# Long filter and two dense layers on one core: the second step in pairs of octets

## The chip, the cores and the metric

The kernel runs on one core of a Trainium2 chip. The metric is the device time of one execution in microseconds, lower is better. Before the change the median of 3 runs is 1322.25 us (1322.2 to 1323.78).

## The reference

A long convolution by FFT over 12480 positions and 128 channels, a gate with x, and then two dense layers on the 12480 tokens (128 to 2048 to 128). Cut to what matters:

```python
h_filt = (np.maximum(pos_emb @ w1, 0.0) @ w2) * np.exp(-0.01 * pos)[:, None]   # filter, 64 rows to 128 channels
y = irfft(rfft(x * v, 2 * S) * rfft(h_filt, 2 * S))[:S]                          # causal convolution
x = x * y
h = x @ w_in;  x = (h * np.clip(h + 3, 0, 6) / 6) @ w_out                        # first dense layer
h = x @ w_in2; x = np.where(h > 0, h, np.exp(np.minimum(h, 0)) - 1) @ w_out2     # second dense layer
```

The weights come as 64-bit floats; the kernel converts them to 32 bits itself.

## The kernel before, in words

**The four steps of the convolution.** The transform has length 179 x 128 and is done in four steps of small matrix products. The first step makes spectra along 98 rows, for 32 groups of channels of the signal (`first_u`) and 16 groups of filter rows (`first_r`). The second step works on 90 frequencies k, in octets: `OCTETS` has 11 octets of 8 and a last one of 2. The third (`third_main`, `third_rest`) and the fourth step (`fourth`, 17 blocks) go back to positions. From about 251 us on the two dense layers run, in units of 512 tokens by 256 hidden columns, and fill the rest of the time.

**The second step, per octet o.** `second_r(o)` (line 450): eight 128x128 products on TensorE turn the filter rows by the table `gm`, and ScalarE copies the result back (line 455). `second_h(o)` (line 457): the filter rows, 64 wide, are expanded to 128 channels by `w2`: two products of 64 contraction rows for each k, into two PSUM buffers `hr[0]` and `hr[1]`; ScalarE copies each (line 466) and makes a negated third copy (line 467) into `hss[o % 2]`. `second_u(o, hf)` (line 469): for each half hf of the channels, eight 128x128 products turn the signal's spectrum by the same table into one PSUM buffer `z`. `second(o, hf, z)` (line 478): VectorE makes two products of z with the expanded filter (line 487) into a pair of buffers of `mms`; GpSimd adds the two (line 492) back into the spectrum. `mms` has two such pairs, used in turn.

**PSUM.** `bank(name, shape, tag)` gives a buffer of 128 x 1024 floats under one of two tags, "px" and "py", each with two buffers in turn. In the second step `second_r` and `second_h` use "px" and `second_u` uses "py". A `second_h` takes both buffers of its tag.

**Tables.** `load_gm0(n)` requests a table group of four k on SP's queue into one of eight places; an octet has two groups, so four octets' tables are present.

**The weight conversion.** `weight_steps` is a generator with 34 steps: the first requests three raw blocks, the second begins block 0, and each of the 32 others finishes one block k. Such a step is three VectorE operations (clamp, line 289; lines 291 and 292), one on GpSimd (line 295), a request for block k+3 on SP (line 262), two ScalarE operations that begin block k+1 (lines 277 and 278), and a store of block k-1 on ScalarE's queue (line 272). `convert(n)` adds n to a counter and issues a step for each whole one. Three steps come in the first step of the transform, 18 in the second, four in the third and nine in the fourth. In `second` the call stands between the two products and their sum. In the third and fourth step a raw request is held until the next `bunch` and goes out behind its other requests.

**Order.** The schedule is written out by hand: each engine executes in the order of the program text. There is no planner.

Of the kernel before, what the change touches and what calls it, by code (L numbers as in the profile page):

```python
# [18 lines left out]
S, D, FO, FF = 12480, 128, 64, 2048  # L19

ZERO = 10398
N1, N2 = 179, 128
# [113 lines left out]
def tile_kernel(ctx, tc, xc, vc, xT, posT, w1_d, w2_d, moe_w, t1_d, gm_d, cs_d, ti_d, rows_d, column_d, ratio_d, outT):  # L136
# [11 lines left out]
    def bank(name, shape, tag=None):  # L148
        if tag is None:
            turn[0] += 1  # L150
            tag = "px" if turn[0] % 2 else "py"
        return ps.tile(shape, F32, tag=tag, name=name)
# [9 lines left out]
    OCT = 8  # L162
# [61 lines left out]
    GN = 8  # L224
# [75 lines left out]
        store(len(jobs) - 1)  # L300

    weights = weight_steps(JOBS, cut(cv, 2 * WC, 3), cut(cv[:, 6 * WC:], WC, 2), cut(cv[:, 8 * WC:], WC, 4))
    RATE = (0.75, 0.65)
    due = [0.0]

    def convert(n):
        due[0] += n
        while due[0] >= 1:
            due[0] -= 1
            next(weights, None)  # L310
# [18 lines left out]
    NC = D // DC  # L329
# [90 lines left out]
    for kind, n in order:  # L420
        if kind:
            first_r(n)
            if n == NR // 2:
                nc.sync.dma_start(cs, cs_d)
                nc.sync.dma_start(w2s, w2_d)
            if n in GM_AT:
                load_gm0(GM_AT.index(n))
        else:
            first_u(us.pop(0), n)
            if n + LOOK < NC:  # L430
                us.append(signal(n + LOOK))
            convert(n >= NC - 3)
    load_gm0(GN - 1)
    lctx.close()
    bctx = ctx.enter_context(ExitStack())
# [11 lines left out]
    def gm_of(k):  # L447
        return gms[k // KC % GN][:, k % KC]

    def second_r(o):  # L450
        k0, nk = OCTETS[o]
        r = bank("r", [128, OCT, N2], "px")
        for j in range(nk):
            nc.tensor.matmul(r[:, j], lhsT=Rk[:, k0 + j], rhs=gm_of(k0 + j), start=True, stop=True)  # L454
        nc.scalar.copy(Rk[:, k0:k0 + nk], r[:, :nk])

    def second_h(o):
        k0, nk = OCTETS[o]
        hr = [bank("h", [128, OCT, D], "px") for r in range(2)]
        for j in range(nk):  # L460
            for r in range(2):
                p = slice(r * FO, (r + 1) * FO)
                nc.tensor.matmul(hr[r][:, j], lhsT=Rk[p, k0 + j], rhs=w2s[p], start=True, stop=True)  # L463
        hs = hss[o % 2]
        for r in range(2):
            nc.scalar.copy(hs[:, :nk, r], hr[r][:, :nk])
        nc.scalar.mul(hs[:, :nk, 2], hs[:, :nk, 1], -1.0)

    def second_u(o, hf, tag="py"):
        k0, nk = OCTETS[o]  # L470
        z = bank("z", [128, OCT, D], tag)
        for j in range(nk):
            nc.tensor.matmul(z[:, j], lhsT=gm_of(k0 + j), rhs=spectrum(hf, k0 + j, 1)[:, :, 0], start=True, stop=True)  # L473
        return z
# [3 lines left out]
    def second(o, hf, z, size=OCT, rate=0):  # L478
        k0, nk = OCTETS[o]
        for a in range(0, nk, size):  # L480
            n = min(size, nk - a)
            m1, m2 = (m[products[0] % 2][:, :, :n] for m in mms)
            products[0] += 1
            h = hss[o % 2][:, a:a + n, :, hf * HD:(hf + 1) * HD]
            flat = h[:, :, 0].unsqueeze(3).to_broadcast([128, n, HD, 2])
            for mm, h in ((m1, flat), (m2, h[:, :, 1:].rearrange("p k r d -> p k d r"))):
                nc.vector.tensor_tensor(  # L487
                    out=mm.rearrange("p d k r -> p k d r"),
                    in0=z[:, a:a + n].rearrange("p k (d r) -> p k d r", r=2), in1=h, op=ALU.mult,
                )  # L490
            convert(rate)
            nc.gpsimd.tensor_tensor(  # L492
                out=spectrum(hf, k0 + a, n), in0=m1, in1=m2[:, :, :, ::-1], op=ALU.add
            )

    def third_main(hf, s0, n, tag=None):
        q = bank("q", [128, 2, 4 * N2], tag)
        for j in range(n):
            for r in range(2):
                for p in range(2):  # L500
                    mm = nc.tensor.matmul(  # L501
                        q[p * HD:(p + 1) * HD, r, j * HN:(j + 1) * HN], lhsT=AuM[hf][:, s0 + j, :, r], rhs=csr[:, r, p],
                        start=True, stop=True,
                    )
                    if j <= 4:
                        anchor[0] = mm
        qs = half(q, n * HN)
        for o, op in enumerate((ALU.subtract, ALU.add)):
            nc.vector.tensor_tensor(
                out=main[hf][:, o, :, s0:s0 + n].rearrange("p g e t -> p e g t"),  # L510
                in0=q[:, 0, :n * HN].rearrange("p (e g t) -> p e g t", e=n, t=2),
                in1=qs.rearrange("p (e g t) -> p e g t", e=n, t=2), op=op,
            )
# [44 lines left out]

    mains = groups([8] * 8)
    turn[0] = 1  # L560
    for o in range(2):
        second_r(o)
        convert(1)
    for o in range(last + 1):
        if o == 0:
            z = second_u(o, 0)
            second_h(o)
            convert(1)
        else:
            second_h(o)  # L570
            z = second_u(o, 0)
        if 0 < o < last:
            second_r(o + 1)
        rate = RATE[0] if o < last - 1 else 0
        second(o, 0, z, rate=rate)
        if o == last:
            third_main(1, *mains[0], "px")
        second(o, 1, second_u(o, 1), rate=rate)
        for n in range(2 * (o > 0)):
            load_gm0(2 * (o - 1) + GN + n)  # L580
    bctx.close()
    lds = cctx.enter_context(tc.tile_pool(name="ldi", bufs=1, reuse_waits="tile"))
    held[0] = True
# [169 lines left out]
    for i, banks in enumerate(BATCHES):  # L753
        if i < len(ahead):
            y, parts, widths = ahead[i]
        else:
            y = new_y(i)
            parts, widths = fourth(i, y)
            parts[0]()
        parts[1]()  # L760
        if bunches.get(i) or i in bunches and pending:
            bunch(*bunches[i])
        o = START.get((banks[0][0], 1), 0)
        if len(set(widths)) == 1:
            n, w = len(widths), widths[0]
            z = xp[:, o:o + n * w].rearrange("p (b n) -> p b n", n=w)
            nc.vector.tensor_tensor(out=z, in0=y[:, :n, :w], in1=z, op=ALU.mult)
        else:
            for b, w in enumerate(widths):
                nc.vector.tensor_tensor(out=xp[:, o:o + w], in0=y[:, b, :w], in1=xp[:, o:o + w], op=ALU.mult)  # L770
                o += w
        if i == 2:
            nc.scalar.copy(x0[:, 0], xp[:, :TT])
        if i in (13, 14, 15):
            split_w(*early[i - 13])
        if i == 3:
            nc.vector.tensor_tensor(out=x0[:, 1], in0=xp[:, :TT], in1=x0[:, 0].bitcast(F32), op=ALU.subtract)
        if i < 15:
            convert(RATE[1])
    assert next(weights, "done") == "done"  # L780
    cctx.close()
    wp = ctx.enter_context(tc.tile_pool(name="wp", bufs=1, reuse_waits="tile"))
# [211 lines left out]
```

## Time and profile before

| what | us |
|---|---|
| median of 3 runs | 1322.25 |
| the profiled execution | 1321.99 |
| its span, first to last instruction | 1320.2 |
| TensorE busy | 1312.2 (99%) |
| VectorE busy | 1134.5 (86%) |
| ScalarE busy | 1006.0 (76%) |
| GpSimd busy | 411.7 (31%) |

The granted TensorE clock is 1.00 in all stretches read here. In the trace PE is TensorE's products and PEld its weight loads, DVE is VectorE, ACT ScalarE, POOL GpSimd, and SPq the queue of requests on SP. A float32 product appears as two instructions. The end of a PE instruction is modelled, so groups of products are best placed by the starts of their weight loads. A part in square brackets is idle time of the engine before the row and what ended it.

### The profile page before, as it was taken

Reading aid. Unit: us, or ns where it says so; the run is one execution under the profiler, and the core shown is the slowest. Engines: PE = TensorE matmul, PEld = TensorE weight load, DVE = VectorE, ACT = ScalarE, POOL = GpSimd, SP = SyncE. Lnnn points to the kernel's source line nnn. Section 1 sums busy time; section 2 is a strip of 40 time slices with the busy share of each in tenths; the row PEclk is TensorE's granted clock in tenths of the full one; section 3 lists DMA queues with packets and bytes.
Section 4 is the critical chain, followed back from the end, with each engine's and each line's share of the span. In section 5 each row is a group of like instructions: output and inputs, shape, how many; then the busy total and the mean of one; then the engine's idle time right before and its main releaser. Section 6 shows DMA issues by size and latency. Waiting matters only on the chain.

```text
span 1320.2 us, 23005 instructions
## 1 busy us (share of the span) xinstructions
PE 1312.2 (99%) x9184; PEld 1127.2 (85%) x9184; DVE 1134.5 (86%) x1209; ACT 1006.0 (76%) x1210; POOL 411.7 (31%) x319
## 2 busy tenths in 40 slices
PE   9999999999999999999999999999999999999998
PEld 9999999888888888888888888888888888888898
DVE  6769877789988888888888888888888888898897
ACT  5677663588877888788877887788778878887776
POOL 1027741334222222333222222222223233222223
PEclk9999999999999999999999999999999999999999
DMA  8944447510000000000000000000000000000000
GB/s 266 266 129 148 133 141 236 180 48 17 9 8 6 4 8 8 9 1 9 9 9 0 8 9 8 1 9 8 8 1 9 8 9 1 8 8 9 8 9 12
DMA packets 33676, 58.80 MB, mean 45 GB/s; under 512 B 3962, under 2 KB 10272, under 8 KB 33568
## 3 DMA queue, kind: packets, MB, share of 16 engines
q1 hardware_dynamic: 28816, 53.07, 13.2%
q10 hardware_dynamic: 4752, 4.26, 0.9%
q8 instruction: 72, 1.18, 0.4%
q14 instruction: 36, 0.29, 0.1%
HBM read 46.73 MB, written 10.58 MB: 43 GB/s over the span
## 4 chain that ended last, share of the span: by engine, by line
PE 92%; DVE 2%; issue 2%; DMA 1%; ACT 1%; POOL 1%; SPq 0%; ACTq 0%; POOLq 0%; DVEq 0%
PE h L867 39%; PE o L911 39%; PE pa L401 4%; PE y L677 3%; PE z L473 2%; PE q L501 2%; PE r L454 1%; PE h L463 1%; PE q L539 1%; DMA uv<-in_xc 1%; DMA qb<-in_posT 0%; POOL a L880 0%; DVE qb L487 0%; ACT gs L896 0%; DVE au L487 0%
## 5 line engine op out<-in xcount | busy, mean ns | idle before, releaser
L911 PE MATMUL o<-gs,w 128*128 128x512 f32 (+1 forms) x2400 | 566.0, 384 | 0.9 <-POOL w L814 0.5
L911 PEld LDWEIGHTS o<-gs,w 128*128 128x128 f32 x2400 | 445.1, 188 | 86.7 <-DVE gs L901 1.0
L880 POOL TENSOR_SCALAR a<-a 128x1024 f32<-128x1024 f32 (+1 forms) x200 | 295.9, 1480 | 706.7 <-ACT a L879 706.5
L901 DVE TENSOR_TENSOR gs<-g,gs 128x1024 fp32r<-128x1024 f32 (+1 forms) x400 | 482.2, 1205 | 5.3 <-ACT gs L896 4.5
L896 ACT CAST gs<-g 128x1024 fp32r<-128x1024 f32 (+1 forms) x400 | 410.1, 1025 | 52.7 <-DVE g L888 51.3
L888 DVE SCALAR_TENSOR_TENSOR g<-a,h 128x1024 f32<-128x1024 f32 (+1 forms) x200 | 238.8, 1194 | 117.5 <-ACT a L877 117.2
L867 PE MATMUL h<-x,w 128*128 128x512 f32 (+1 forms) x1200 | 298.1, 384 | 0.2 <-ACT a L879 0.2
L867 PE MATMUL h<-xs,w 128*128 128x512 f32 (+1 forms) x1200 | 297.9, 384 | 0.0
L879 ACT ACTIVATE a<-h 128x1024 f32<-128x1024 f32 (+1 forms) x200 | 201.4, 1007 | 89.6 <-PE h L867 88.3
L867 PEld LDWEIGHTS h<-xs,w 128*128 128x128 f32 x1200 | 223.1, 188 | 44.7 <-DVE g L888 0.4
L867 PEld LDWEIGHTS h<-x,w 128*128 128x128 f32 x1200 | 223.0, 188 | 43.7 <-issue 0.5
L877 ACT ACTIVATE a<-h,bounds 128x1024 f32<-128x1024 f32 (+1 forms) x200 | 219.0, 1095 | 50.3 <-PE h L867 50.3
L890 DVE SCALAR_TENSOR_TENSOR g<-a,h 128x1024 f32<-128x1024 f32 (+1 forms) x200 | 237.6, 1188 | 0.2 <-POOL a L880 0.2
L295 POOL TENSOR_TENSOR cv<-cv 128x256 int32<-128x256 int32 x32 | 23.4, 732 | 121.0 <-DVE cv L292 111.8
L401 PE MATMUL pa<-tab,qb 98*64 98x180 f32 x512 | 41.6, 316 | 0.1
L401 PEld LDWEIGHTS pa<-tab,qb 98*64 98x64 f32 x512 | 37.8, 138 | 2.6 <-ACT qb L405 0.4
L277 ACT ACTIVATE cv<-cv 128x256 int32<-128x256 uint32 x32 | 14.3, 446 | 23.7 <-DMA cv<-in_mw 17.7
L814 POOL TENSOR_TENSOR w<-w 128x256 fp32r<-128x256 f32 x26 | 19.2, 742 | 37.9 <-DVE gs L901 16.7
L677 PE MATMUL y<-qb 128*64 128x97 f32 (+3 forms) x896 | 30.9, 248 | 0.1
L677 PEld LDWEIGHTS y<-qb 128*64 128x64 f32 (+1 forms) x896 | 28.9, 137 | 1.9 <-issue 0.3
L492 POOL TENSOR_TENSOR qb<-qb,bp 128x1024 f32<-128x1024 f32 (+1 forms) x12 | 26.9, 2240 | 3.9 <-DVE bp L487 3.9
L843 ACT COPY y<-o 128x512 f32<-128x512 f32 (+1 forms) x25 | 14.5, 578 | 17.5 <-PE o L911 17.5
(98 smaller groups left out, 866.1 us busy)
## 6 DMA issues: line engine op xcount, KB each, us to landing
cv<-in_mw SPq DMA_DIRECT2D x32, 256.0 KB
uv<-in_xc SPq DMA_DIRECT2D x32, 196.0 KB
out_T<-y SPq DMA_DIRECT2D x23, 256.0 KB
qb<-in_gm SPq DMA_DIRECT2D x22, 256.0 KB
au<-in_xT SPq DMA_DIRECT2D x16, 268.0 KB
qb<-in_ti SPq DMA_DIRECT2D x14, 294.0 KB
w_scratch<-cv ACTq DMA_DIRECT2D x32, 128.0 KB
w<-w_scratch SPq DMA_DIRECT2D x16, 256.0 KB
```

The lines of the kernel that those rows point to most:

```text
L401: nc.tensor.matmul(pa[f * HN:(f + 1) * HN, j, :2 * NK], lhsT=src(j, f), rhs=table[:, f], start=True, stop=True)
L492: nc.gpsimd.tensor_tensor(out=spectrum(hf, k0 + a, n), in0=m1, in1=m2[:, :, :, ::-1], op=ALU.add)
L677: anchor[0] = nc.tensor.matmul(y[c * HD:(c + 1) * HD, b, off:off + w], lhsT=lhsT, rhs=rhs[:, H1 - w:], start=(b, c) in fresh, stop=done, s ...
L867: nc.tensor.matmul(h[:, j], lhsT=wslice(2 * m - 2, a, 2 * u + j), rhs=x[:, b], start=i == 0, stop=i == 2)
L877: paced[0] = nc.scalar.activation(a, h, AF.Relu, bias=three)
L879: nc.scalar.activation(a, h, AF.Exp)
L880: nc.gpsimd.tensor_scalar(a, a, 1.0, 0.0, op0=ALU.min, op1=ALU.max)
L888: last_dve[0] = nc.vector.scalar_tensor_tensor(g, a, 6.0, h, op0=ALU.min, op1=ALU.mult)
L890: last_dve[0] = nc.vector.scalar_tensor_tensor(g, a, -1.0, h, op0=ALU.add, op1=ALU.max)
L896: nc.scalar.copy(t[:, 0], g)
L901: last_dve[0] = nc.vector.tensor_tensor(out=t[:, 1], in0=g, in1=t[:, 0].bitcast(F32), op=ALU.subtract)
L911: nc.tensor.matmul(o[:, :WID[t]], lhsT=wslice(2 * m - 1, a, 2 * u + j), rhs=gs[:, b, j], start=u == 0 and j == 0 and i == 0, stop=u == NU ...
```

## The change

The octets of the second step are taken in pairs (a, a+1). Both `second_h` come first, one in each tag, then four `second_u` with their `second`; `second_r(a+2)` comes after the first two of them and `second_r(a+3)` after the last. The tags change places from pair to pair: a = 0, 4, 8 have p = "px" and q = "py", a = 2, 6, 10 the reverse. The last pair consists of octet 10 and the short octet 11. The requests for the tables of octets a+4 and a+5 follow the octet whose places they take. The conversion steps are dealt out anew: five in the first step, 15 in the second (none, one or a third at the end of a pair), four in the third and ten in the fourth.

```diff
-    RATE = (0.75, 0.65)
+    RATE = 0.67
@@ first step
-            convert(n >= NC - 3)
+            convert(n >= NC - 5)
@@ second step: second_r, second_h and second_u take their tag as an argument
-    for o in range(2):
-        second_r(o)
-        convert(1)
-    for o in range(last + 1):
-        if o == 0:
-            z = second_u(o, 0)
-            second_h(o)
-            convert(1)
-        else:
-            second_h(o)
-            z = second_u(o, 0)
-        if 0 < o < last:
-            second_r(o + 1)
-        rate = RATE[0] if o < last - 1 else 0
-        second(o, 0, z, rate=rate)
-        if o == last:
-            third_main(1, *mains[0], "px")
-        second(o, 1, second_u(o, 1), rate=rate)
-        for n in range(2 * (o > 0)):
-            load_gm0(2 * (o - 1) + GN + n)
+    tags = ("px", "py")
+    for o in range(2):
+        second_r(o, tags[o])
+        convert(1)
+
+    def load_tables(o):
+        for n in range(2):
+            load_gm0(2 * o + n)
+
+    for a in range(0, last, 2):
+        p, q = tags[::1 - (a & 2)]
+        second_h(a, p)
+        convert(a == 0)
+        second_h(a + 1, q)
+        convert(1 if a + 1 < last else 0)
+        second(a, 0, second_u(a, 0, p))
+        second(a, 1, second_u(a, 1, p), rate=1 if a + 1 < last else 0)
+        load_tables(a + 4)
+        if a + 1 < last:
+            second_r(a + 2, q)
+            second(a + 1, 0, second_u(a + 1, 0, q))
+            z = second_u(a + 1, 1, p)
+            second_r(a + 3, p)
+            second(a + 1, 1, z)
+            convert(a in (2, 6))
+            load_tables(a + 5)
+    second(last, 0, second_u(last, 0, "px"))
+    third_main(1, *mains[0], "px")
+    second(last, 1, second_u(last, 1, "py"))
@@ fourth step
-            convert(RATE[1])
+            convert(RATE)
```

## Rows read from the trace of the kernel before

**Rows 1.** Busy time by stretch: us, busy (count) per engine, granted clock, DMA.

```profile
102.50:156.00 53.50, 53.50 (x564) 51.74 (x563) 48.38 (x60) 36.24 (x49) 41.98 (x26) 1.00 0.48 148
300.00:1320.20 1020.20, 1016.38 (x4593) 851.41 (x4591) 898.18 (x812) 811.54 (x863) 299.61 (x206) 1.00 0.02 7
```

**Rows 2.** Timeline of weight loads, octet 4: start, duration, engine, line, operation.

```profile
112.05 1.86 PEld L463 LDWEIGHTS h<-qb 64*128 64x128 f32 x32
114.03 1.90 PEld L473 LDWEIGHTS z<-qb 128*128 128x128 f32 x16
115.85 1.86 PEld L454 LDWEIGHTS r<-qb 128*128 128x128 f32 x16
117.64 1.89 PEld L473 LDWEIGHTS z<-au,qb 128*128 128x128 f32 x16
119.66 1.86 PEld L463 LDWEIGHTS h<-qb 64*128 64x128 f32 x32
```

**Rows 3.** Timeline of VectorE and GpSimd around octets 4 and 5.

```profile
114.06 2.38 POOL L492 TENSOR_TENSOR qb<-qb,bp 128x1024 f32<-128x1024 f32 x1
...
115.43 1.17 DVE L289 TENSOR_SCALAR cv<-cv 128x256 f32<-128x256 f32 x1
...
118.23 2.38 POOL L492 TENSOR_TENSOR au<-qb,au 128x1024 f32<-128x1024 f32 x1
...
120.64 1.23 DVE L487 TENSOR_TENSOR qb<-z,qb 128x1024 f32<-128x1024 f32 x1 [0.95 <-POOL au L492]
...
121.79 1.25 DVE L487 TENSOR_TENSOR au<-z,qb 128x1024 f32<-128x1024 f32 x1
122.95 0.29 DVE L289 TENSOR_SCALAR cv<-cv 128x256 f32<-128x256 f32 x1
...
123.60 0.43 DVE L292 SCALAR_TENSOR_TENSOR cv<-cv 128x256 int32<-128x256 int32 x1
...
124.17 0.73 POOL L295 TENSOR_TENSOR cv<-cv 128x256 int32<-128x256 int32 x1 [1.23 <-DVE cv L292]
```

**Rows 4.** Timeline: a product behind its `second_u`, and `second_u` behind a product.

```profile
136.90 2.09 PE L473 MATMUL z<-qb 128*128 128x128 f32 x16
...
139.13 1.23 DVE L487 TENSOR_TENSOR qb<-z,bp 128x1024 f32<-128x1024 f32 x1 [0.17 <-PE z L473]
...
166.63 1.24 DVE L487 TENSOR_TENSOR au<-z,qb 128x1024 f32<-128x1024 f32 x1
...
167.92 0.53 PEld L473 LDWEIGHTS z<-au,qb 128*128 128x128 f32 x4 [0.50 <-DVE au L487]
```

**Rows 5.** Timeline of ScalarE and of TensorE's waits, first octets.

```profile
78.11 0.43 ACT L277 ACTIVATE cv<-cv 128x256 int32<-128x256 uint32 x1
...
78.92 0.82 ACT L405 ACTIVATE au<-pa 128x512 f32<-128x512 f32 x2
...
80.60 1.01 ACT L455 COPY qb<-r 128x1024 f32<-128x1024 f32 x1
...
86.18 1.93 ACT L466 COPY qb<-h 128x1024 f32<-128x1024 f32 x2 [1.77 <-PE h L463]
...
88.14 1.06 ACT L467 ACTIVATE qb<-qb 128x1024 f32<-128x1024 f32 x1
...
90.53 1.90 PEld L473 LDWEIGHTS z<-qb 128*128 128x128 f32 x16 [0.52 <-DVE bp L487]
...
100.61 1.86 PEld L454 LDWEIGHTS r<-qb 128*128 128x128 f32 x16 [0.56 <-ACT qb L466]
```

**Rows 6.** Timeline where the fourth step meets the dense layers.

```profile
246.31 0.44 ACT L277 ACTIVATE cv<-cv 128x256 int32<-128x256 uint32 x1 [4.93 <-DMA cv<-in_mw]
...
247.99 1.43 DVE L292 SCALAR_TENSOR_TENSOR cv<-cv 128x256 int32<-128x256 int32 x1
...
249.34 1.83 DVE L767 TENSOR_TENSOR au<-y,au 128x780 f32<-128x780 f32 x2
...
254.31 2.59 DVE L888 SCALAR_TENSOR_TENSOR g<-a,h 128x1024 f32<-128x1024 f32 x2 [1.04 <-ACT a L877]
...
255.58 1.22 PEld L867 LDWEIGHTS h<-xs,w 128*128 128x128 f32 x6 [0.16 <-DVE g L888]
```

More of the change, by code (lines that the diff above doesn't have):

```diff
@@ L448, in gm_of, with second_r @@
         return gms[k // KC % GN][:, k % KC]
-    def second_r(o):
+    def second_r(o, tag):
         k0, nk = OCTETS[o]
-        r = bank("r", [128, OCT, N2], "px")
+        r = bank("r", [128, OCT, N2], tag)
         for j in range(nk):
@@ L455, in second_r, with second_h @@
         nc.scalar.copy(Rk[:, k0:k0 + nk], r[:, :nk])
-    def second_h(o):
+    def second_h(o, tag):
         k0, nk = OCTETS[o]
-        hr = [bank("h", [128, OCT, D], "px") for r in range(2)]
+        hr = [bank("h", [128, OCT, D], tag) for r in range(2)]
         for j in range(nk):
@@ L467, in second_h, with second_u @@
         nc.scalar.mul(hs[:, :nk, 2], hs[:, :nk, 1], -1.0)
-    def second_u(o, hf, tag="py"):
+    def second_u(o, hf, tag):
         k0, nk = OCTETS[o]
```

## The prediction

> **What bounds the kernel now.** I read the busy time by stretch first. In seven middle octets of the second step TensorE is busy all 53.5 us of 53.5, VectorE 48.4, GpSimd 42.0; in the dense layers from 300 us on TensorE is busy 1016.4 of 1020.2 [rows 1]. The reader is to see two things: TensorE sets the time on both sides of the change, so each microsecond it loses or gains here reaches the end; and VectorE has only a tenth to spare beside it.
>
> Second the timeline of one octet, by the starts of TensorE's weight loads [rows 2]. `second_h` takes 1.98 us, `second_u` 1.82, `second_r` 1.79, the other `second_u` 2.02: 7.61 together. The same 16 products of `second_u` cost 0.20 more when `second_h` follows, and `second_h` itself, whose loads span 1.86, lasts 0.12 to 0.14 longer until the next group starts. So the change between 128-row and 64-row products costs about 0.34 us an octet.
>
> Third VectorE and GpSimd in the same octet [rows 3]. Products stand 1.15 and 1.16 us apart. One waits 0.95 us for a GpSimd sum: the two buffer sets of `mms` alternate, so a product waits for the sum of two products earlier, which takes 2.38. A conversion step queues between a product and its sum: clamp, two more operations, 0.65 from the first's start to the last's, which takes 0.43; GpSimd's part follows 0.14 later and takes 0.73; only then does the sum start. A clamp that meets a running sum ends 0.16 after it (114.06 + 2.38 against 115.43 + 1.17).
>
> **The change, in the pairs.** There are two tags of two PSUM buffers. One `second_h` takes both buffers of a tag; two in a row take all four. So the second of a pair cannot start before the last products of the pair before it, those of `second_u(a+1, 1)`, have left their buffer. This wait is new; before, `second_h` and `second_r` used "px" alone and VectorE's lag sat in "py".
>
> *What it removes.* Six pairs of switches instead of twelve: 6 x 0.34 = 2.0 us. Of waits of TensorE in the old step, three go: 0.52 and 0.56 in the first octets [rows 5], 0.50 in the last [rows 4], 1.6 together.
>
> *What it adds.* I follow one pair from its first product, T = 0. The pairs of products start at 0 and 2.31 and the fourth product is through at 4.62. The first sum starts at 1.15 + 1.25 + 0.14 = 2.54 and ends at 4.92, so the clamp ends at 5.08. From a clamp's end to the last operation's start is 0.36 (123.24 to 123.60): 5.44, end 5.87, GpSimd's part 6.01 to 6.74, the second sum 6.74 to 9.12. VectorE meanwhile starts the next pair at 5.79 and has its fourth set of products due at 8.10, but these need the buffer of the second sum: 9.15. They end at 9.15 + 1.15 + 1.25 = 11.55. TensorE starts 0.05 after such an end (166.63 + 1.24, then 167.92) [rows 4]: 11.60. The product can start 2.23 after its `second_u` starts (136.90 to 139.13) [rows 4], so the second expansion of the next pair may start 13.83 after `second_u(a, 0)`. TensorE alone would be there after four times 1.82, twice 1.79, 0.20 and 1.86: 12.92. So it waits 0.9 us per pair, and two switches saved give 0.34 back: a loss of 0.6. The loop closes: 1.98 + 2.23 + 11.60 = 15.81 against 2 x 7.61 = 15.22. Nothing gives it back, since the wait delays `second_u` and so the next T by as much.
>
> Behind the waiting expansion on TensorE stand the four products of the pair; ScalarE's copies wait for it too, but have time.
>
> The six boundaries, one by one. Expansions 5 and 9: 0.9 each. After octets 3 and 7 a third conversion step queues before T, and its last operation may be held by the pair's last sum, as one is by another GpSimd operation in rows 6: 0 to 0.15, I take 0.15, so expansion 7 waits 1.05. The last boundary is shorter on TensorE, since `second_r(11)` has two rows for eight: expansion 10 comes after 4 x 1.82 + 1.79 + 0.45 + 0.20 = 9.72, its buffer at 5.79 + 2.40 + 0.05 + 2.23 = 10.47, a wait of 0.75, with the 0.15 again 0.9, and expansion 11 then waits 13.83 - 10.47 - 1.86 = 1.5.
>
> The first boundary needs the start. ScalarE takes two steps more before `second_r(0)`, 0.81 each (78.11 to 78.92, two operations) [rows 5]; with the gaps between evictions the first copy moves from 80.6 to about 81.4. Then in its queue: copy 0.9, step 0.9, copy, step, two copies 1.93, negation 1.0, step: 88.9. VectorE has the four steps issued up to then ahead of its first product, so T is about 89.95, while TensorE would allow 88.5. Expansion 0 waits 0.15 for its copy; 2 waits until T + 8.1, 0.65; 3 until T + 11.4, 1.5. All waits: 0.15 + 0.65 + 1.5 + 0.9 + 1.05 + 0.9 + 0.9 + 1.5 = 7.5. The second step: 7.5 - 2.0 - 1.6 = +3.9. At its end the last sum (two products behind two full ones on GpSimd) comes some 0.1 after TensorE is ready for the third step: +4.0. Bounds: +2.5 if the chain is 0.3 shorter per pair, which is 0.06 at each of its five handovers, +5.4 if the clamp at a pair's end loses its place, below.
>
> One handover isn't in the trace: a clamp queued where one GpSimd sum ends and the next is about ready. The nearest rows are a clamp stretched to 1.17 by a running sum [rows 3] and a last operation stretched to 1.43 beside another GpSimd operation [rows 6]. I take it that the clamp goes first: it is due at 11.46, the next sum at 11.55 + 0.14 = 11.69. The other end is that it waits a whole sum, 2.38 in each of two pairs, of which VectorE's idle time before T covers the most: 0 to 1.4 in all. The Trainium skill, "SBUF — State Buffer", section "SBUF: two separate sides", has it that whichever of the two engines starts first holds the shared ports for its whole instruction. By that rule too the clamp would go ahead and the 1.4 be nothing; no row here shows a clamp due so close before a sum.
>
> **The steps moved.** Of 34, five instead of three come in the first step, 15 instead of 18 in the second, ten instead of nine in the fourth. In the first, VectorE and GpSimd are free; ScalarE's share is priced above. The three weight requests pass one table request on SP and land many us before use: nothing (0 to 0.3). The table requests of the second step come after `second_u` of the octet whose place they take, a whole pair, 15 us, before their `second_r`: nothing. In the fourth, the last step stands one block later, behind a request grouped after two others. Before, ScalarE waits 4.93 for such a load at 246.31 and the product of block 14 comes at 249.34, all hidden; VectorE's slack before the first gate is 1.04, and TensorE's fourth unit already waits 0.16 for that gate [rows 6]. A step of 1.0, plus up to 1.0 if an operation of it is stretched as the one of 1.43 is, now falls in that slack: 0 to 1.0, I take 0.5.
>
> Sum: 1321.99 (profiled execution, span 1320.2) + 4.0 + 0.5 = 1326.5; the runs' median is 0.26 above that execution, less than the sum resolves. I forecast 1326.5.
>
> **Rivals.** *TensorE keeps its pace* (faster). One mechanism: the fourth products don't wait for the second sum. It decides at 0.9 us: if the last products end by T + 10.7 instead of 11.6, no full pair waits. VectorE alone would be at 10.5. Against it: the 0.95 wait for a sum in rows 3, which is this very wait. Then -2.0 - 1.6, with 0.8 left in the start: 1319.2. The Trainium skill, "TensorEngine Tiling (Array Packing)", section "Key Properties", says that a change of tiling mode drains TensorE; by that alone the time would fall by the 2.0. The trace agrees on the price of a switch.
>
> *Half the waits.* The start and the last pair overlap better than my queues say, the rest as worked: waits of about 4.5 instead of 7.5, so +0.9 and the gate's 0.5: 1323.4. For it: ScalarE's lateness at the start is put together from gaps, not read.
>
> *The handover is lost*, and the gate takes its upper end: +1.4 and +0.5, 1328.4. For it: sums come back to back at every pair's end. Against it: VectorE idles there.
>
> *It doesn't do what it says:* two expansions in a row still switch, since they belong to different buffers; 2.0 isn't saved, 1328.5. All switches seen are between shapes, so I count it with the case before.
>
> **How the numbers follow.** Forecast 0.50 (1325 to 1327.7), half the waits 0.22 (1321.5 to 1325), lost handover or switches 0.14 (1327.7 to 1329.5), TensorE's pace 0.14 (1318.5 to 1321). A measurement tells 0.2%, 2.6 us, from no change. Slower than 1324.9: 0.64 less some of the forecast's edge, 0.62; faster than 1319.6: the last case, counted whole, 0.14; the same: 0.24. The range leaves out the last case and the top of the third: 1321.0 to 1329.0; the forecast's own is 1325 to 1327.7.
>
> **What would show it.** Right: `second_h` as two groups with no 0.34 between them in a pair; TensorE idle before every odd expansion from 3 on, released by the products of the octet before, 0.9 us in the middle, 1.5 at the ends; a product of each odd octet waiting about 1.0 for a sum; pairs of 15.8 us. Wrong: pairs of 14.9 with no idle, or TensorE waiting for ScalarE or a table. The dense layers should start 4 to 5 us later and last as long as before.

## The result and the profile after

The changed kernel takes 1330.37 us (1329.36 to 1332.82, 4 runs) against 1322.66 for the kernel before on the same chip (4 runs): a ratio of 1.0064, 95% interval 1.0053 to 1.0076, slower by 7.7 us. Its profiled execution takes 1330.22 us, span 1328.4. The direction came as forecast, the size did not: 1326.5 was predicted and the range ended at 1329.0.

The busy time by stretch, as in [rows 1]: a stretch of the second step of the same length, here from the start of octet 3's expansion (`second_h`) on, then the dense layers.

```profile
102.88:156.38 53.50, 51.62 (x542) 50.21 (x543) 47.36 (x53) 35.30 (x46) 37.27 (x22) 1.00 0.34 112
300.00:1328.40 1028.40, 1024.61 (x4629) 858.24 (x4628) 904.91 (x818) 819.31 (x870) 303.57 (x211) 1.00 0.02 8
```

TensorE, busy for all of this stretch before, is now idle 1.9 us in one as long. In the dense layers it is as full as before. The weight loads of one pair, octets 4 and 5 (start, duration, engine, line, operation, idle time before it), answer to [rows 2]:

```profile
115.93 2.08 PEld L463 LDWEIGHTS h<-qb 64*128 64x128 f32 x34
118.61 1.86 PEld L463 LDWEIGHTS h<-qb 64*128 64x128 f32 x30 [0.59 <-DVE au L487]
120.58 1.90 PEld L473 LDWEIGHTS z<-qb 128*128 128x128 f32 x16
122.41 1.89 PEld L473 LDWEIGHTS z<-au,qb 128*128 128x128 f32 x16
...
131.67 2.08 PEld L463 LDWEIGHTS h<-qb 64*128 64x128 f32 x34
135.02 1.86 PEld L463 LDWEIGHTS h<-qb 64*128 64x128 f32 x30 [1.27 <-DVE au L487]
```

The second expansion of a pair waits for VectorE's last product of the pair before: TensorE is idle 0.59 here and 1.27 in the next pair. Between the two expansions there is no 0.34 for a switch. Two expansions that don't wait take 3.78 until `second_u` starts (82.28 to 86.06 in experiment 3), so the wait of a pair is 120.58 - 115.93 - 3.78 = 0.87 here, 1.55 and 0.86 in the two pairs that follow. VectorE and GpSimd over one pair, as in [rows 3]:

```profile
107.09 1.23 DVE L487 TENSOR_TENSOR qb<-z,qb 128x1024 f32<-128x1024 f32 x1 [1.14 <-PE z L473]
...
109.62 2.39 POOL L492 TENSOR_TENSOR qb<-qb,bp 128x1024 f32<-128x1024 f32 x1 [2.79 <-DVE bp L487]
...
111.69 0.47 DVE L289 TENSOR_SCALAR cv<-cv 128x256 f32<-128x256 f32 x1
...
112.52 0.43 DVE L292 SCALAR_TENSOR_TENSOR cv<-cv 128x256 int32<-128x256 int32 x1
...
113.78 2.37 POOL L492 TENSOR_TENSOR au<-qb,au 128x1024 f32<-128x1024 f32 x1
...
116.18 1.23 DVE L487 TENSOR_TENSOR qb<-z,bp 128x1024 f32<-128x1024 f32 x1 [0.94 <-POOL au L492]
117.32 1.23 DVE L487 TENSOR_TENSOR au<-z,bp 128x1024 f32<-128x1024 f32 x1
118.47 0.28 DVE L289 TENSOR_SCALAR cv<-cv 128x256 f32<-128x256 f32 x1
...
118.70 2.37 POOL L492 TENSOR_TENSOR au<-qb,au 128x1024 f32<-128x1024 f32 x1 [0.21 <-DVE au L487]
118.79 2.43 DVE L291 TENSOR_SCALAR cv<-cv 128x256 int32<-128x256 int32 x1
```

This is the chain of the prediction, from T = 107.09: first sum at T + 2.53 (predicted 2.54), clamp through at 5.07 (5.08), last operation at 5.43 (5.44), second sum at 6.69 (6.74), the fourth products wait 0.94 for it and end at 11.46 (11.55). The last rows are new: the clamp goes ahead of the last sum, the next operation does not, and takes 2.43 for 0.30.

The start, ScalarE and TensorE, as in [rows 5]:

```profile
82.44 0.45 ACT L277 ACTIVATE cv<-cv 128x256 int32<-128x256 uint32 x1 [0.77 <-DMA w_scratch<-cv]
...
84.35 1.86 PEld L463 LDWEIGHTS h<-qb 64*128 64x128 f32 x32 [0.30 <-ACT qb L455]
85.47 0.44 ACT L277 ACTIVATE cv<-cv 128x256 int32<-128x256 uint32 x1 [1.17 <-DMA cv<-in_mw]
...
86.32 1.93 ACT L466 COPY qb<-h 128x1024 f32<-128x1024 f32 x2
...
87.38 1.88 PEld L473 LDWEIGHTS z<-qb 128*128 128x128 f32 x16 [1.16 <-ACT qb L466]
...
91.24 1.22 DVE L487 TENSOR_TENSOR qb<-z,qb 128x1024 f32<-128x1024 f32 x1
```

ScalarE waits for a store and for a raw block that has not landed, with the copy of the first expansion behind both; TensorE then waits for the copy, and VectorE's first product starts at 91.24. Last the end of the second step and the first gate of the dense layers, [rows 4] and [rows 6]; lines behind the second step are numbered nine higher here:

```profile
173.88 0.52 PEld L473 LDWEIGHTS z<-au,qb 128*128 128x128 f32 x4
...
174.97 0.41 DVE L487 TENSOR_TENSOR bp<-z,bp 128x256 f32<-128x256 f32 x1
...
175.50 2.63 PEld L501 LDWEIGHTS q<-cs,au 128*64 128x64 f32 x82 [1.11 <-PE z L473]
175.53 4.15 PE L501 MATMUL q<-cs,au 128*64 128x64 f32 x128 [0.94 <-DVE bp L487]
...
254.49 1.40 DVE L292 SCALAR_TENSOR_TENSOR cv<-cv 128x256 int32<-128x256 int32 x1
...
258.25 1.48 DVE L292 SCALAR_TENSOR_TENSOR cv<-cv 128x256 int32<-128x256 int32 x1
...
260.66 2.61 PEld L876 LDWEIGHTS h<-xs,w 128*128 128x128 f32 x12 [0.77 <-DVE au L776]
...
264.23 1.91 PEld L876 LDWEIGHTS h<-xs,w 128*128 128x128 f32 x9 [0.96 <-DVE g L897]
```

Where the 8.2 us between the spans lie, by starts of weight loads: from the first `second_r` to the last `second_u` 95.46 for 89.42 (+6.04); from there to the first 28 loads in a row of line 539 (`third_rest`) 6.89 for 5.91 (+1.0); from there to the dense layers, third and fourth step, 77.90 for 77.63 (+0.27); dense layers 1069.73 for 1068.73 (+1.0); the first `second_r` 0.08 earlier.

### The profile page after: what moved, and what is told of

The parts are those of the page before. It is cut to its first block, busy times and chain, and to the rows that moved or that the text cites. A ratio compares the mean times of both kernels' runs of the same rounds, so it can differ in the third digit from the quotient of the medians.

```text
span 1328.4 us, 23043 instructions
## 1 busy us (share of the span) xinstructions
PE 1313.3 (99%) x9184; PEld 1127.3 (85%) x9184; DVE 1138.0 (86%) x1209; ACT 1006.2 (76%) x1210; POOL 412.6 (31%) x319
## 3 DMA queue, kind: packets, MB, share of 16 engines
q8 instruction: 72, 1.18, 0.4%
## 4 chain that ended last, share of the span: by engine, by line
PE 85%; DVE 4%; DMA 3%; issue 3%; POOL 2%; ACT 2%; SPq 0%; ACTq 0%; DVEq 0%; POOLq 0%
PE o L920 39%; PE h L876 38%; PE pa L401 4%; PE q L501 2%; DMA cv<-in_mw 2%; PE q L539 1%; DVE qb L487 1%; DVE au L487 1%; POOL au L492 1%; DVE cv L291 1%; PE y L686 1%; DMA qb<-in_posT 1%; PE z L473 0%; DMA tab<-in_rows 0%; PE h L463 0%
## 5 line engine op out<-in xcount | busy, mean ns | idle before, releaser
L463 PE MATMUL h<-qb 64*128 64x128 f32 x360 | 24.9, 279 | 5.5 <-DVE au L487 4.2
```

## The experiments

One table for all. "Second step" runs from the first `second_r` to the last `second_u`, "start" from there to the first `second_u` of octet 2; a pair is from `second_u(a, 0)` to the next pair's, without and with a third conversion step ahead of it. Each ratio is against the kernel before on the same chip (medians there 1322.03 to 1322.66).

| kernel | us | ratio (95%) | second step | start | pair, 2 and 3 steps |
|---|---|---|---|---|---|
| before | 1322.25 | | 89.42 | 19.67 | 15.22 (two octets) |
| after | 1330.37 | 1.0064 (1.0053 to 1.0076) | 95.46 | 26.44 | 15.72, 16.42 |
| 1 tail's tag | 1328.17 | 1.0047 (1.0030 to 1.0064) | 95.82 | 26.78 | 15.73, 16.42 |
| 2 step later | 1328.30 | 1.0049 (1.0034 to 1.0064) | 93.30 | 25.32 | 15.37, 16.14 |
| 3 three first | 1327.15 | 1.0040 (1.0025 to 1.0055) | 93.43 | 24.41 | 15.72, 16.08 |
| 4 gate | 1329.59 | 1.0059 (1.0044 to 1.0074) | 95.32 | 26.29 | 15.73, 16.40 |
| 5 later and swapped | 1327.49 | 1.0037 (1.0023 to 1.0051) | 92.41 | 25.35 | 14.88, 16.16 |
| 6 step ahead of sum | 1328.67 | 1.0047 (1.0032 to 1.0062) | 94.21 | 25.67 | 15.71, 15.91 |
| 7 two steps in a row | 1334.11 | 1.0088 (1.0073 to 1.0103) | 102.06 | 24.62 | -, 17.05 |
| 8 = 1, 4, 5, 6 | 1325.20 | 1.0023 (1.0013 to 1.0033) | 91.31 | 24.57 | 14.90, 15.92 |
| 9 = 8, three first | 1326.15 | 1.0031 (1.0019 to 1.0043) | 92.37 | 23.47 | -, 15.94 |
| 10 = 7, store late | 1332.48 | 1.0075 (1.0060 to 1.0090) | 98.67 | 24.09 | -, 16.51 |
| 11 after, narrow steps | 1322.98 | 1.0003 (0.9994 to 1.0012) | 88.45 | 24.26 | 14.84, 14.88 |
| 12 before, narrow steps | 1320.86 | 0.9990 (0.9980 to 0.9999) | 88.36 | | 15.24 (two octets) |

The start of before is not comparable: there neither `second_r(3)` nor octet 3's expansion stands ahead of the first `second_u` of octet 2.

**1. The tail's buffer.** The second `third_main` takes its buffer from "py", where the next one in turn is that of `second_u(10, 1)`, and the third from "px":

```diff
-        third_main(1, *mains[k], "px" if k == 1 else None)
+        third_main(1, *mains[k], "py" if k == 1 else "px")
```

> The changed kernel, but of the third step's products the second group (third_main 1) takes its buffer from py and the third group from px. Theory A: in the changed kernel that second group waits about 1.0 us because its px buffer still holds second_u(11, 0), whose VectorE products wait for GpSimd's last full sums; in py the buffer is free (its products end some 0.1 us before TensorE arrives), so TensorE's idle time there goes, the third step starts 0.9 us earlier, and the time is 1329.4. Theory B (the third step's start is set by GpSimd's last sum, and the wait only moves to third_rest): the start of third_rest doesn't move by more than 0.2 us, 1330.3. Nothing before 171 us should change by either.

```profile
174.27 0.52 PEld L473 LDWEIGHTS z<-au,qb 128*128 128x128 f32 x4
174.92 2.17 PEld L501 LDWEIGHTS q<-cs,au 128*64 128x64 f32 x68
...
254.34 2.73 PE L686 MATMUL y<-qb 52*64 52x98 f32 x78 [1.18 <-issue]
```

Weight loads and a product of this kernel: the group follows the last `second_u` after 0.65 instead of 1.62, so the wait was for that buffer. In this execution the fourth step gave 0.8 of it back, at a product that waits for nothing that the profile shows. The median fell by 2.2, more than the 0.9 to 1.0 expected; the intervals of the two ratios overlap, so the rows are the reading and not the time.

**2. The step in the middle, later.** The conversion step of `second(a, 1)` goes into `second(a+1, 0)`.

```diff
-        second(a, 1, second_u(a, 1, p), rate=1 if a + 1 < last else 0)
+        second(a, 1, second_u(a, 1, p))
...
-            second(a + 1, 0, second_u(a + 1, 0, q))
+            second(a + 1, 0, second_u(a + 1, 0, q), rate=1)
```

> The changed kernel, but the conversion step in the middle of a pair is issued one product later: between the products and the sum of (a+1, 0) instead of those of (a, 1). Nothing is added or left out. Theory A (the second expansion of the next pair waits for the fourth products, these for the second sum, and that for the conversion step queued before it on GpSimd): the second sum now starts at T + 4.9, the fourth products end at T + 10.6 instead of 11.6, and TensorE would be at the expansion only at about T + 10.7: the waits of 0.8 at expansions 5 and 9 go (under 0.2), the 1.5 at expansion 7 falls to about 0.6, those at 2 and 3 together from 2.4 to 1.4, those at 10 and 11 from 2.5 to 1.3. Sum -4.5: 1325.9. Theory B (VectorE has too little time in a pair, whatever the order of its queue): the pairs stay at 15.7 us, 1330.4 within 0.5.

```profile
106.20 1.23 DVE L487 TENSOR_TENSOR qb<-z,qb 128x1024 f32<-128x1024 f32 x1 [0.34 <-PE z L473]
...
109.41 1.90 PEld L473 LDWEIGHTS z<-qb 128*128 128x128 f32 x16
...
111.64 1.23 DVE L487 TENSOR_TENSOR qb<-z,bp 128x1024 f32<-128x1024 f32 x1 [0.77 <-ACT cv L278]
...
117.37 1.86 PEld L463 LDWEIGHTS h<-qb 64*128 64x128 f32 x30 [0.24 <-DVE au L487]
```

The waits named in the expectation fell by 1.9 together instead of 4.5. In a plain pair, one without a third step, the rows give the reason: the third product now comes at T + 5.44, and that is 2.23 after its own `second_u`, which stands behind `second_r(a+2)` on TensorE. (The profile names ScalarE as its releaser, whose operation ended 0.10 before; 2.23 is the distance of [rows 4].) One releaser went and the next stood 0.5 behind it. In the pairs behind a third step the third product does come at T + 4.94, as expected; but at each pair's end the clamp now meets the sum ahead and takes 1.16 for 0.28 (117.22), with its next operation held as before, and expansion 7 still waits 1.28, the last two 2.5.

**3. Three steps in the first step,** as before, the two others at the pairs' ends.

```diff
-            convert(n >= NC - 5)
+            convert(n >= NC - 3)
...
-            convert(a in (2, 6))
+            convert(a > 0)
```

> The changed kernel, but three conversion steps instead of five stand in the first step, and the two go to the ends of the pairs of octets 4 and 8, so each pair but the first has three. Theory A (the start is late because ScalarE's begin operations wait for raw blocks and stores that can't arrive faster: 1.17 and 0.77 us of DMA waits, with two steps more in its queue before the first copies): those waits go, and second_u(2, 0) starts about 1.3 us earlier after second_r(0) than in the changed kernel (104.86 - 78.42 = 26.4 us there). The third step at the ends of two more pairs costs about 0.7 each, as after octets 3 and 7: the pair from second_u(6, 0) to second_u(8, 0) grows from 15.7 to 16.4. Net about 0: 1330.4. Theory B (the transfers don't matter; the start is VectorE's four steps before the first product, which are the same number here): the start moves by less than 0.4 us and the time is 1331.5.

```profile
83.45 0.44 ACT L277 ACTIVATE cv<-cv 128x256 int32<-128x256 uint32 x1
...
84.37 1.93 ACT L466 COPY qb<-h 128x1024 f32<-128x1024 f32 x2
...
86.06 1.89 PEld L473 LDWEIGHTS z<-qb 128*128 128x128 f32 x16
```

The start is 2.0 shorter (24.41 for 26.44): ScalarE finds every raw block landed, and its copy comes 2.0 earlier. The start varies by itself, 25.67 to 26.78 in four kernels that have it unchanged (after, 1, 4, 6), so 1.3 to 2.4 is what this shows. The time, 1327.15, is 3.2 below the one expected: the pairs behind a third step take 16.08 where 16.4 was expected, and the dense layers take 1068.77, 1.0 less than in the changed kernel, though the edit does not touch them.

**4. The gate.** The last step of the fourth step of the transform goes to the third.

```diff
-    RATE = 0.67
+    RATE = 0.65
...
+        convert(k == 5)
```

> The changed kernel, but with nine conversion steps in the fourth step, spread as before the change, and five in the third (one more, at its fifth main group). Theory A (the last conversion step, one block later, pushes VectorE's products of blocks 14 to 16 and the first gates, for which TensorE waits): the waits at the start of the dense layers fall back to those of before (0.16 at the fourth unit), and from the first unit to the end it takes 1068.7 us as before, not 1069.7. The third step grows by 0 to 0.3. Time 1329.5. Theory B (the dense layers' start is late for another reason, such as the order of the weight requests): no change, 1330.4.

The dense layers last 1068.71, as before (1068.73), with waits of 0.16 and 0.21 where the changed kernel has 0.77 and 0.96. The whole gain is inside the interval of its ratio; the length of the dense layers is the reading. But the dense layers also take 1068.77 in kernel 3 and 1068.86 in kernel 1, which lack this edit. Kernel 1, its last operation of the conversion and the first load of the dense layers:

```profile
257.58 1.47 DVE L292 SCALAR_TENSOR_TENSOR cv<-cv 128x256 int32<-128x256 int32 x1
...
258.84 3.96 PEld L876 LDWEIGHTS h<-xs,w 128*128 128x128 f32 x18
```

That operation starts 1.26 ahead of the dense layers here and 1.18 in kernel 3, but 0.42 in the changed kernel (258.25 to 258.67). In kernels 2, 5 and 6 it is 0.62 to 0.77, and the dense layers take 1069.24 to 1069.58; in kernel 11 it is 1.07, and they take 1069.12. In the kernels with nine steps in the fourth step (4, 7, 8, 9, 10) it is at least 2.4, and they take 1068.55 to 1068.78. So the edit takes the loss away; without it the loss is 0.0 to 1.0 and goes with how late the last step comes.

**5. Later, and `second_u` first.** Experiment 2, with `second_u(a+1, 0)` put ahead of `second_r(a+2)`.

```diff
+            z = second_u(a + 1, 0, q)
             second_r(a + 2, q)
-            second(a + 1, 0, second_u(a + 1, 0, q))
+            second(a + 1, 0, z, rate=1)
```

> The step stands one half octet later, as in the second experiment, and second_u(a+1,0) is put ahead of second_r(a+2), so the third product no longer waits for a second_u that stands behind second_r. Theory A (each wait of an odd expansion is when the fourth products end, and these wait for the first sum, then for their second_u): the third product starts at T+4.95 instead of T+5.43, the fourth products end at about T+10.55, and TensorE comes to the next pair's second expansion at T+10.7. So expansions 5 and 9 wait 0 to 0.1 (0.80 in the changed kernel, 0.44 in the second experiment), expansion 7 waits 0.7 to 0.9 because the third step at the end of octet 3 is still there, the start waits about 1.2 and the last two expansions 1.3 to 2.0. The time is 1326.5 to 1327.3, from 1328.3. Theory B (VectorE simply has too much to do in a pair, whatever the order): the waits and the time are those of the second experiment, 1328.3.

Pairs without a third step take 14.88: no wait is left there, and what TensorE needs alone is seen, two old octets less one pair of switches (15.22 - 0.34). The time, 1327.49, is 0.2 above the range expected. The pair with a third step still waits, and VectorE and GpSimd ahead of it show why:

```profile
117.56 2.44 POOL L492 TENSOR_TENSOR au<-qb,au 128x1024 f32<-128x1024 f32 x1
117.81 2.35 DVE L291 TENSOR_SCALAR cv<-cv 128x256 int32<-128x256 int32 x1
```

**6. The third step ahead of the last sum.**

```diff
-            second(a + 1, 1, z)
-            convert(a in (2, 6))
+            second(a + 1, 1, z, rate=a in (2, 6))
```

> The changed kernel with one edit: the third conversion step after octets 3 and 7 is issued between the last two products and the last sum instead of behind that sum. Theory A (the step's second operation is stretched to 2.43 us because the last sum on GpSimd holds the buffers both engines reach): that operation takes about 0.3 again, the fourth product of the next pair is earlier by 0.6 to 0.7, expansion 7 waits about 0.8 instead of 1.48, expansions 10 and 11 together about 1.9 instead of 2.52, and the time falls by 0.8 to 1.3, to about 1329.3. Theory B (a step costs its VectorE time at a pair's end wherever it stands): nothing changes, 1330.4.

```profile
117.04 0.29 DVE L291 TENSOR_SCALAR cv<-cv 128x256 int32<-128x256 int32 x1
...
118.63 2.43 POOL L492 TENSOR_TENSOR au<-qb,au 128x1024 f32<-128x1024 f32 x1
118.85 2.49 DVE L292 SCALAR_TENSOR_TENSOR cv<-cv 128x256 int32<-128x256 int32 x1
```

The third step's second operation (line 291) takes 0.29 again, and expansion 7 waits 1.04 instead of 1.55. But the next step's last operation now meets the sum and takes 2.49, and the last two expansions wait as before (2.5), where 1.9 was expected: the stretch moved to the step behind. Of the 1.25 that the second step is shorter, 0.77 is in the start, which this edit does not touch.

**7. All at once, two steps in a row.** Three steps in the first step, 18 in the second: per pair one in `second(a+1, 0)` and two in `second(a+1, 1)`, and none between the expansions and the first product but in the first pair; with the swap of 5, the tag of 1 and the rate of 4. The last of these edits:

```diff
-            second(a + 1, 1, z)
-            convert(a in (2, 6))
+            second(a + 1, 1, z, rate=2)
```

> All causes undone together in the paired order: three steps in the first step of the transform (rest of ScalarE's queue free), the fourth step's rate as in the kernel before, one step in the pair's third half octet with second_u ahead of second_r, two steps in the fourth half octet and none behind a pair, the tail's buffer in the other tag. Theory A (the loss is these waits and nothing else; two expansions in a row do save 0.34 us per pair of switches): the waits of expansions 5, 7 and 9 go to 0 to 0.2 each, the start to about 1.5, the last two expansions to about 1.5, the tail's and the gate's waits go, so the second step takes 87.5 to 89 us against 89.4 before: 1320 to 1322, at or below the kernel before. Theory B (pairs lose whatever the order, since one more step beside two sums makes VectorE late by as much elsewhere): 1325 or more.

1334.11 is slower than the changed kernel. The number lies in theory B's range, but the rows show a path that neither theory had. GpSimd, ScalarE and TensorE at a pair's start:

```profile
117.84 0.72 POOL L295 TENSOR_TENSOR cv<-cv 128x256 int32<-128x256 int32 x1 [1.09 <-DVE cv L292]
118.59 0.33 ACTq L272 DMA_DIRECT2D w_scratch<-cv  x1
118.96 1.93 ACT L466 COPY qb<-h 128x1024 f32<-128x1024 f32 x2 [1.56 <-POOL cv L295]
...
120.02 1.89 PEld L473 LDWEIGHTS z<-qb 128*128 128x128 f32 x16 [2.28 <-ACT qb L466]
```

The bound changed engine: the second step's store on ScalarE's queue waits for GpSimd's part of the first, which waits for VectorE, the copy of the expansion stands behind the store, and TensorE waits 2.28 for the copy.

**8 and 9. The losses mended together.** Kernel 8 joins experiments 1, 4, 5 and 6 (five steps stay in the first step). Kernel 9 takes that back to three and deals the two others to octets 1 and 5:

```diff
-            convert(n >= NC - 5)
+            convert(n >= NC - 3)
...
-            second(a + 1, 1, z, rate=a in (2, 6))
+            second(a + 1, 1, z, rate=a < 8)
```

> The fifth experiment (step half an octet later, second_u ahead of second_r) together with the sixth (third step issued ahead of the last sum), the first (the tail's buffer in the other tag) and the fourth (one step from the fourth step of the transform to the third). Still five steps in the first step. Theory A (the losses are separate waits of TensorE and add up): from 1327.5, expansion 7 waits about 0.6 instead of 1.2, the last two expansions 0.3 less, the tail 0.65 less, the dense layers last 1.0 less: about 1325.0, at most 1326. Theory B (what is gained before the dense layers is given back where TensorE waits for the last blocks' tables, as the first experiment's profile hinted): 1326 to 1327, with the third and fourth step longer by what the second step got shorter.

> The eighth experiment's kernel with only three steps in the first step of the transform, and the two others dealt to octets 1 and 5, between the last products and the last sum, so that every full pair but the last has three steps, never two in a row at one place. Theory A: the start is 1.3 to 2.0 us shorter, as in the third experiment; a third step in a pair costs 0 to 0.6 in each of two pairs: 1323 to 1325, within 0.2% of the kernel before. Theory B (three steps in a pair are what made the seventh experiment lose): pairs of 16 to 17 us and 1327 or more.

Kernel 8 comes at 1325.20, some 5 us below the changed kernel, as expected if the losses are separate. Its second step is 1.9 longer than before, its tail (5.90) and its dense layers (1068.68) as before, and third and fourth step take 78.59 for 77.63. Kernel 9 gains 1.1 at the start, where TensorE still waits 1.1, at expansion 3, and loses 1.04 in each of two pairs that now have a third step (15.94 for 14.90): 1326.15, a miss of 1.2 to the bad side of theory A, though not theory B's 1327. A pair can't hide a third step even where no two stand in a row at one place.

**10. The store one step later** in kernel 7.

```diff
-            store(k - 1)
+            store(k - 2)
...
+        store(len(jobs) - 2)
```

> The seventh experiment's kernel (two steps in a row in the fourth half octet, pairs of 17.05 us) with one edit: each step stores the block of two steps before instead of one. In the seventh, ScalarE's copy of the first expansion stands behind the second step's store, which waits for GpSimd's part of the first step, and the next second_u waits 3 us for that copy. Theory A (that queue is the cause): the copy comes 1.0 to 1.6 us earlier, pairs take 15.6 to 16.1 us and the time falls from 1334.1 to 1328 to 1330. Theory B (two steps in a row make VectorE itself late, or ScalarE waits for the raw block's landing): pairs stay at 16.7 to 17.1 and the time above 1332.

```profile
117.02 0.44 ACT L277 ACTIVATE cv<-cv 128x256 int32<-128x256 uint32 x1 [1.53 <-DMA w_scratch<-cv]
...
118.98 1.90 PEld L474 LDWEIGHTS z<-qb 128*128 128x128 f32 x16 [1.73 <-ACT qb L467]
```

Pairs of 16.51 lie between the two expectations, and the time, 1332.48, in theory B's. The wait for GpSimd is gone and another has its place on the same queue: the next step's first operation waits 1.53 for a store that has not left its buffer, since four buffers with a later store are one too few. So in both kernels TensorE waits for what stands on ScalarE's queue; that the queue alone costs these pairs their 2.2 us over 14.88 is not shown, since the edit could not clear it.

**11 and 12. The steps without their width,** in both orders: in the second step the three VectorE operations and GpSimd's work on one column of 256, everything else is kept (those weights are not converted).

```diff
-            w = raws[k % 3].rearrange("p (n t) -> p n t", t=2)
+            w = raws[k % 3].rearrange("p (n t) -> p n t", t=2)[:, :wide[0]]
```

> The changed kernel, in which the 15 conversion steps of the second step do their three VectorE operations and the GpSimd one on a single column instead of 256 (so those weights are not converted, which leaves out that part of the computation); requests, ScalarE's operations and stores stay. Theory A (what the pairs lose is VectorE's and GpSimd's time for the steps ahead of the sums; the two switches saved per pair are real): TensorE waits in no full pair, pairs are 14.9 us, the start still waits 1 to 2 for ScalarE and its raw blocks, the last two expansions 1.0 to 1.5 together; the second step is 4 to 5.5 us shorter than in the changed kernel (95.5 to about 90.5), and the time about 1325 to 1326.5. Theory B (two expansions in a row must wait for all four buffers of PSUM, steps or not): the odd expansions still wait 0.5 or more, and the time stays above 1328.

> The kernel before with the same cut: its 18 conversion steps of the second step on one column. Theory A (the old order hides the steps, since VectorE's lag sits in the buffers of the other tag): only the three old waits shrink, octets stay at 7.61, and the second step is 0.5 to 1.6 us shorter than the 89.4 of before: 1320.8 to 1322. Theory B (the steps cost both orders alike, and the pairs lose for another reason): it falls by 4 us or more as well, to 1318 or less.

The pairs' second step falls by 7.0, more than expected, the old order's by 1.06. Without the width both take the same, 88.45 and 88.36: full pairs have no wait (14.84 to 14.88), and the 2.0 us of switches are spent on waits at the start, 1.7, and in the last pair, about 0.9. So the tags alone cost nothing in a full pair; the steps ahead of the sums do. Even so the paired kernel is 2.1 behind the old order, 1.0 of it the tail of experiment 1 and 0.4 in the dense layers. VectorE and GpSimd of kernel 11:

```profile
115.14 2.36 POOL L492 TENSOR_TENSOR au<-qb,au 128x1024 f32<-128x1024 f32 x1
115.28 2.24 DVE L292 SCALAR_TENSOR_TENSOR cv<-cv 128x1 int32<-128x1 int32 x1
```

An operation on one column takes 2.24, to the end of the sum, where it takes 0.16 elsewhere in this kernel (109.73): it is held, not slowed.

## Why the prediction was wrong in size

**Right.** TensorE sets the time; six pairs of switches go; the odd expansions wait for the last products of the pair before, and these for a sum. Every step of the chain lies within 0.1 us of its prediction, and so do the waits of a plain pair (0.87 and 0.86 for 0.9) and its length (15.72 for 15.81). The rival of TensorE's own pace had its deciding point right too: in kernel 5 the last products of a plain pair end at T + 10.62, early enough for the 10.7 asked, and the pair takes 14.88.

**Wrong: the start.** "Then in its queue: copy 0.9, step 0.9, copy, step, two copies": the queue was taken as always fed. Its operations wait 0.77 for a store and 1.17 for a raw block, TensorE waits 1.16 for ScalarE, which the prediction had named as a sign of being wrong, and T is 91.24 for 89.95. The three weight requests were priced at nothing since they "land many us before use"; the waits up to expansion 3 are 1.41 at the first `second_u`, 0.18 at the next `second_r` and 2.46 at expansions 2 and 3, 4.05 instead of 2.30. Experiment 3 shows that about half of this, 2.0 (1.3 to 2.4), hangs on the two steps added there: without them the wait of 1.41 is gone, and ScalarE's for the raw block with it. The 2.0 that stay at expansions 2 and 3 there are near the 2.15 predicted for these two.

**Wrong: the third step at a pair's end.** The prediction asked whether the clamp goes first, and for the rest said that "its last operation may be held by the pair's last sum", 0.15. The clamp does go first. The operation behind it starts 0.09 after the sum and is held for all of it, 2.43 for 0.30; VectorE's idle time covers that in a plain pair, not where a second step queues behind: expansion 7 waits 1.55 for 1.05, and the last two together about 2.5 for 2.4. The Trainium skill, "SBUF — State Buffer", section "SBUF: two separate sides", says that of two instructions that need the port pair shared by VectorE and GpSimd the one that starts second is blocked for the other's whole instruction; the rows agree, and 2.24 for one column agrees best. I applied that rule to the clamp and not to the operation behind it.

**Wrong: the end of the step.** The last sum "comes some 0.1 after TensorE is ready for the third step": the second `third_main` waits about 1.0, for VectorE's products (174.97) to leave the PSUM buffer of `second_u(11, 0)`. Moving a tag to the last octet moved a wait into the third step, and I had followed the tags only up to the octets' end. Experiment 1 shows it.

**Wrong: the gate's size.** "0 to 1.0, I take 0.5": in the traced execution it is 1.0, the upper end, and the dense layers, which were to last as long as before, are longer by it. Experiment 4 takes it away. In each of the two steps ahead of the gate one operation is held, 1.40 and 1.48; but in kernel 1, with 1.43 and 1.47, the loss is 0.1, so the held operations alone don't make it. In these kernels it goes with how late the last step comes: a wait of 0.0 to 1.0, where the prediction took a fixed share of a step's price.

The misses add up: 2.1 in the second step (its waits, some 9.8, are 2.3 above those predicted, whose terms add up to 7.55; 1.75 of it is the start and 0.5 the third step), 0.9 at its end, 0.5 at the gate and 0.27 in the third and fourth step, less 0.08: 3.7, which is 8.2 less the 4.5 predicted.

**Open.** Third and fourth step take 77.36 to 79.20 in these kernels, at places where TensorE waits for nothing shown; I did not settle why. Nor is it shown why kernel 3's pairs behind a third step are shorter than the changed kernel's. No version here that converts all the weights beats the kernel before; kernel 8 comes nearest, 0.13 to 0.33% slower.

## What to carry to other kernels

When two groups of products are put next to each other to save a switch, list what each buffer of both tags waits for through to the first use after the loop, for the saving is certain and small and every wait counts in full. A step that "fits into idle time" must be followed on each queue that it touches, VectorE, GpSimd, ScalarE's and the requests, and with the operation behind the one that gets its place. When a mended wait gains less than its size, look for the next releaser close behind it: here it was there three times.

## What the runs showed of the hardware

A request of 256 KB took some 5 us among others. The raw block for which ScalarE waits until 85.47 in the changed kernel was requested at 80.32 on SP's queue; from 76 to 103 us the DMA engines moved 171 GB/s (99 in the kernel before, where ScalarE waits for no raw block there).

The clock. In kernel 7 TensorE is busy 1.85 of the 6 us before 171 us, waiting for ScalarE; its busy times by stretch (granted clock third from the end):

```profile
165.00:171.00 6.00, 1.85 (x26) 1.47 (x22) 5.18 (x8) 1.93 (x4) 4.09 (x4) 0.95 0.34 116
171.00:179.00 8.00, 7.83 (x58) 7.70 (x60) 3.35 (x3) 3.04 (x6) 3.97 (x3) 0.61 0.13 44
```

The granted clock is then 0.61 over 8 us, most of it at the lower level of 1.2 GHz, and 16 loads of `second_u` that take 1.90 elsewhere take 3.48. In the changed kernel, busy 11.81 of the 13 us from 168 to 181, the clock stays at 1.00. So part of what experiment 7 loses is this, 1.3 to 1.6 for each of two groups, and not the queue itself. Kernel 10 has it too: busy 3.75 of the 6 us before 167 us, then a clock of 0.57 over 8 us. The pairs of 17.05 and 16.51 stand before that, at 1.00.
